# Pairs of steps share their VectorE instructions, the parts of a transform alternate, and a row is written later

## The chip, the cores and the metric

The kernel runs on one core of a Trainium2 chip. The metric is the device time of the execution in microseconds, lower is better. PE is TensorE (the matrix engine), DVE is VectorE, ACT is ScalarE, POOL is GpSimd, SP is SyncE, which here only issues DMAs. L480 is line 480 of the kernel before.

## The reference

A two-dimensional Fourier transform of x (batch 8, sequence 3008, width 256), of which the real part is kept, and a feed-forward layer with a squared relu on all 8 x 3008 = 24064 tokens:

```python
X = np.fft.fft(x, axis=1)
X = np.fft.fft(X, axis=2)
x = X.real.astype(np.float32).reshape(B * S, D)     # 24064 x 256
h = np.maximum(x @ w_in, 0.0)                       # 24064 x 2048
return (h * h @ w_out).astype(np.float32)           # 24064 x 256
```

## The kernel before

The transform along the width is folded into w_in ahead of the main work: gh[:, 0] and gh[:, 1] are the cosine and sine transforms of w_in (2048 columns in 16 chunks of 128), gh[:, 2] is what turns one into the other sign. So the first product takes two inputs of the sequence transform, zc (cosine, part 0) and zs (sine, part 1), with 128 rows (half of the width) on the partitions and tokens as columns. One column stands for two tokens, the token and its mirror: for one the cosine and sine products are added, for the other they are subtracted. Of width index 128 only a row is left over; it stands in row 0 of zs.

**Windows and steps.** The columns are cut into 25 windows (240, 512, 376, 376, 512, 448, then 512 each, the last 360). The loop over windows `for w` (L679) runs eight steps a window, of two chunks of w_in (256 columns) each. Two forms of a step exist:
- A whole step: `pq` (L725, four matmuls of lines L729 and L730) fills a PSUM tile ph; ACT writes its relu to h1 (L739; there are three h1 buffers) and DVE squares it into h2 (L744), or ACT does (L742). Then `turn` (L732, matmuls L735) changes ph to the mirrored tokens, and relu and square follow again.
- A halved step: `half_q` (L750, matmuls L754) makes the sine product alone, which ACT copies, scaled by -2, to sn (L757). `row_sum` (L769) multiplies the spread row eb by two weights (L774, twice) and adds them to sn (L779). `half_p` (L759, matmuls L763) adds the cosine product, and ACT copies the sum to hd (L766). In the next step `halves` (L782) makes the other sign by hd + sn (L787, mirrored), the maximum with 0 of both (L788), and the square of both into h2 (L789).

A plan (L60, read by `halved` and `plan`) names which steps of a window are halved: 1 to 5, 1 to 4 or 1 to 3, by what else the window has to do; windows 0, 1, 2 and 4 have none. In all, 82 steps are halved. sn uses two buffers in turn, hd the tags tt and tm in turn with two buffers each.

**What runs beside the steps.** `others(s)` (L792) is called in the middle of each step, between its first and its second product on PE. It issues three things: jobs that fold the input of a later batch (mostly DVE), a share of the second product of the window before (`ffn2_steps`, 16 matmuls L618 a step, h2 by w_out; every second step ACT evicts a tile to osb, L633, and SP stores it, L598), and a share of the sequence transform of the next window's columns.

That transform comes in units (batch, e), e = 0 or 1. `z_steps` (L460) gives the jobs of a unit by part (0 for zc, 1 for zs) and half (0 or 1). Each job is one matmul (L480). Both halves of a part go to the same PSUM tile pz: half 0 ends with an ACT copy of pz to es (L485); half 1 begins by overwriting pz and ends with an ACT copy of the plus columns to zc or zs (L489), after which DVE makes the mirrored columns, 2 es - pz (L496, `minus`). A half has 3 jobs where e = 0; where e = 1 it has 4 in part 0 and 6 in part 1. The jobs are listed at L721 in the order (part, half) = (0,0), (1,0), (1,1), (0,1), and spread evenly over the steps lo to hi - 1, usually 0 to 6.

**The row.** `row_spread` (L574) sends row 0 of zs to a DRAM row zr by a DMA of the ACT queue (L579) and from there, spread over 128 partitions, to eb by a DMA of the SP queue (L581). It is called in the window before the one that uses eb, in step hi - 1 (usually 6), when the next window has halved steps.

The order on every engine is the one in which the code issues the instructions; the two PSUM tags of the steps and of pz have two buffers each.

Of the kernel before, what the change touches and what calls it, by code (L numbers as in the profile page):

```python
# [8 lines left out]
F32 = mybir.dt.float32  # L9
# [10 lines left out]
def rev_dim(ap, i):  # L20

    dims = [list(d) for d in ap.ap]
    step, cnt = dims[i]
    dims[i] = [-step, cnt]
    return bass.AP(tensor=ap.tensor, offset=ap.offset + step * (cnt - 1), ap=dims)
# [3 lines left out]
def kernel(  # L29
# [27 lines left out]
    FIRST = [240, 512, 376, 376, 512, 448]  # L57
    R23 = float(2.0 ** 23)

    PLAN = {0: ((1, 2, 3, 4, 5), (0, 6, 7)), 1: ((1, 2, 3, 4), (0, 5, 6)), 2: ((1, 2, 3), (0, 5, 6))}  # L60

    RQ = (1, 3, 5, 0, 2, 4)

# [143 lines left out]
    def table_steps(e):  # L207

        n = unit_cols[e][0]
        nr = 2 if e else 3  # L210
        cos_t = const.tile([P, 2 if e else R, n], F16, name=f"cos{e}")
        sin_t = const.tile([P, 2 if e else R, n], F16, name=f"sin{e}")
        tabs[e] = (cos_t, sin_t)
        vec, vs = (evec, evs) if e else (nvec, nvs)
        st = {}

        def row(h, j):
            return j if e else RQ[3 * h + j]

        def freq():  # L220
            kf = st["kf"] = tmp.tile([P, NE], F32, name="kf", tag="kf")[:, 0:n]
            i = 0
            for k0, kstep, cnt in unit_runs[e][0]:
                nc.vector.tensor_scalar(out=kf[:, i : i + cnt], in0=irow[:, i : i + cnt], scalar1=float(kstep), scalar2=float(k0 - kstep * i), op0=ALU.mult, op1=ALU.add)
                i += cnt

        def args(h):
            t = st["t", h] = tmp.tile([P, 3, NE], F32, name="t", tag="tt")
            for j in range(nr):
                r = row(h, j)  # L230
                if e == 0:
                    nc.scalar.activation(t[:, j, 0:n], st["kf"], AF.Copy, bias=R23, scale=vs[:, r : r + 1])
                else:
                    nc.vector.tensor_scalar(out=t[:, j, 0:n], in0=st["kf"], scalar1=vs[:, r : r + 1], scalar2=R23, op0=ALU.mult, op1=ALU.add)

        def turns(h):
            t = st["t", h]
            nc.vector.tensor_scalar(out=t[:, 0:nr, 0:n], in0=t[:, 0:nr, 0:n], scalar1=-R23, scalar2=-float(S), op0=ALU.add, op1=ALU.mult)

        def mods(h):  # L240
            m = st["m", h] = tmp.tile([P, 3, NE], F32, name="m", tag="tm")
            for j in range(nr):
                r = row(h, j)
                nc.vector.scalar_tensor_tensor(out=m[:, j, 0:n], in0=st["kf"], scalar=vec[:, r : r + 1], in1=st["t", h][:, j, 0:n], op0=ALU.mult, op1=ALU.add)

        def absm(h):
            nc.vector.tensor_scalar(out=st["t", h][:, 0:nr, 0:n].bitcast(I32), in0=st["m", h][:, 0:nr, 0:n].bitcast(I32), scalar1=0x7FFFFFFF, scalar2=None, op0=ALU.bitwise_and)

        def sins(h):
            nc.scalar.activation(sin_t[:, 3 * h : 3 * h + nr, :], st["m", h][:, 0:nr, 0:n], AF.Sin, bias=0.0, scale=wk)  # L250

        def coss(h):
            if e:
# [272 lines left out]
    def run(*jobs):  # L526
        for j in jobs:
            j()
# [45 lines left out]
    def row_spread(w):  # L574

        wn = wins[w][1]
        t = eb[w] = tmp.tile([P, WN], F16, name="eb", tag="kf")
        zr = drp.tile([1, WN], F16, name="zr", tag="zr")
        nc.scalar.dma_start(out=zr[0:1, 0:wn], in_=zwin(w)[1][0:1, 0:wn])  # L579
        src = zr[0:1, 0:wn]  # L580
        nc.sync.dma_start(out=t[:, 0:wn], in_=bass.AP(tensor=src.tensor, offset=src.offset, ap=[[0, P], [1, wn]]))  # L581
# [90 lines left out]
    def halved(w):  # L672

        return plan(w)[0]
# [4 lines left out]
    for w in range(NW):  # L679
# [38 lines left out]
        zj, zl = [], []  # L718
        for u in need[w + 1]:
            zu = z_steps(u)  # L720
            zj += [(zu, 0, 0), (zu, 1, 0), (zu, 1, 1), (zu, 0, 1)]  # L721
        f2 = ffn2_steps(*old) if old else []
        phs = {}

# [18 lines left out]
                return []  # L743
            return [lambda: nc.vector.tensor_tensor(h2[:, 2 * s : 2 * s + 2, sg * wn : (sg + 1) * wn], hv, hv, op=ALU.mult)]  # L744

        two = halved(w)
        by_act = plan(w)[1]
        sns, hds = {}, {}

        def half_q(s):  # L750
            ph = phs[s] = ps_h.tile([P, 2, 512], F32, name="ph", tag="psh")
            for a in range(2):
                f0 = (2 * s + a) * P
                nc.tensor.matmul(ph[:, a, 0:wn], gh[:, 1, f0 : f0 + P], zsw[:, 0:wn], start=True, stop=True)  # L754
            i = ROT[0] % 2
            sn = sns[s] = const.tile([P, 2, 2, WN], F16, name=f"sn{i}", tag=f"w16_{i}")
            nc.scalar.activation(sn[:, 0, :, 0:wn], ph[:, :, 0:wn], AF.Copy, bias=0.0, scale=-2.0)  # L757

        def half_p(s):  # L759
            ph, sn = phs[s], sns[s]  # L760
            for a in range(2):
                f0 = (2 * s + a) * P
                nc.tensor.matmul(ph[:, a, 0:wn], gh[:, 0, f0 : f0 + P], zcw[:, 0:wn], start=False, stop=True, skip_group_check=True)  # L763
            hd = tmp.tile([P, 2, 2 * WN], F16, name="hd", tag=("tt", "tm")[ROT[0] % 2])
            ROT[0] += 1
            nc.scalar.activation(hd[:, :, 0:wn], ph[:, :, 0:wn], AF.Copy, bias=0.0, scale=1.0)  # L766
            hds[s] = hd

        def row_sum(s):  # L769

            sn = sns[s]

            def row(a):
                nc.vector.tensor_scalar(out=sn[:, 1, a, 0:wn], in0=eb[w][:, 0:wn], scalar1=wv[:, 2 * s + a : 2 * s + a + 1], scalar2=None, op0=ALU.mult)  # L774

            return [
                lambda: row(0),
                lambda: row(1),
                lambda: nc.vector.tensor_tensor(sn[:, 0, :, 0:wn], sn[:, 0, :, 0:wn], sn[:, 1, :, 0:wn], op=ALU.add),  # L779
            ]  # L780

        def halves(s):  # L782

            sn, hd = sns[s], hds[s]
            hv = hd[:, :, 0 : 2 * wn]
            return [
                lambda: nc.vector.tensor_tensor(rev_dim(hd[:, :, wn : 2 * wn], 2), hd[:, :, 0:wn], sn[:, 0, :, 0:wn], op=ALU.add),  # L787
                lambda: nc.vector.tensor_scalar(out=hv, in0=hv, scalar1=0.0, scalar2=None, op0=ALU.max),  # L788
                lambda: nc.vector.tensor_tensor(h2[:, 2 * s : 2 * s + 2, 0 : 2 * wn], hv, hv, op=ALU.mult),  # L789
            ]  # L790

        def others(s):  # L792
# [13 lines left out]
        ng = 2 if w == 0 or wins[w - 1][1] < 384 < wn else 1  # L806
        for s0 in range(0, NST, ng):
            ss = range(s0, s0 + ng)
            left = halves(s0 - 1) if s0 - 1 in two else []
            if s0 in two:  # L810
                half_q(s0)
                for j in [j for p in zip(left or [run] * 3, row_sum(s0)) for j in p]:
                    j()
                others(s0)
                half_p(s0)
                continue
            for s in ss:
                pq(s)
            for s in ss:
                run(*(left[0:2] + square(s, 0) + left[2:3]))  # L820
            if s0 == hi - 1 and ng == 1 and w + 1 < NW and halved(w + 1):
                row_spread(w + 1)
            others(s0)
            for s in ss:
                turn(s)
            for s in ss:
                run(*square(s, 1))
            for s in ss[1:]:
                others(s)
            if s0 < hi <= s0 + ng - 1 and w + 1 < NW and halved(w + 1):  # L830
                row_spread(w + 1)
# [33 lines left out]
```

## Time and profile before

| | |
|---|---|
| median of 3 runs | 620.66 us (619.44 to 620.81) |
| the profiled execution | 619.07 us |
| its span in the profile | 617.1 us |
| granted TensorE clock | 0.998 |
| window 13 (313.07 to 338.93): length, busy PE / DVE / ACT | 25.86, 24.77 / 20.72 / 22.39 us |
| window 14 (338.93 to 363.01) | 24.08, 24.08 / 19.14 / 21.37 us |
| window 22 (532.91 to 558.19) | 25.28, 23.85 / 21.20 / 21.49 us |

A window begins with its first product's first matmul and ends with the next window's. Window 13 transforms a unit with e = 1 for a later window and has halved steps 1 to 3; window 14 transforms one with e = 0 and has halved steps 1 to 5; window 22 transforms the last unit, e = 1, which window 23 needs at once, and has steps 1 to 5 halved too. Busy times are sums of durations and can overlap at their ends. In lines of the timeline, the first number is the start in microseconds from the span's start, the second the time that the instruction took (for several, from the first to the last), and the bracket at the end is the idle time of the engine before it and what ended it.

### The profile page before, as it was taken

How to read it: one execution, taken by the hardware profiler on the slowest of the kernel's cores; microseconds unless marked ns; L12 is line 12 of the kernel's file. 1: busy time of each engine (PE TensorE's matmuls, PEld its weight loads, DVE VectorE, ACT ScalarE, POOL GpSimd, SP SyncE). 2: the span in 40 equal slices, each digit the busy share in tenths (PEclk: the TensorE clock that was granted, in tenths of full speed). 3: DMA queues.
4: the chain of work that ended last, by engine and by line, in shares of the span. 5: the costliest groups of instructions: out<-in, count | busy, mean ns of one | idle time of the engine just before them, and what ended most of it. 6: DMA issues, size and time to landing. Idle time of an engine off the chain costs nothing.

```text
span 617.1 us, 11655 instructions
## 1 busy us (share of the span) xinstructions
PE 587.7 (95%) x4400; PEld 424.0 (69%) x4400; DVE 498.6 (81%) x870; ACT 517.6 (84%) x673; POOL 77.3 (13%) x125
## 2 busy tenths in 40 slices
PE   5899999999899999999999999999999999999996
PEld 2456776776677777677776767677776776766785
DVE  7886688696888887969978799768987698797980
ACT  7786788888889889889898898888987988979871
POOL 5352200002001022020011100211000200100000
PEclk9999999999999999999999999999999999999999
DMA  8937121164214522631145311552212411111122
GB/s 145 219 71 144 61 68 35 43 150 104 52 38 83 151 85 57 134 112 59 37 106 121 91 49 46 98 131 81 52 31 66 111 52 44 55 47 42 58 58 65
DMA packets 39593, 50.22 MB, mean 81 GB/s; under 512 B 4572, under 2 KB 33393, under 8 KB 39537
## 3 DMA queue, kind: packets, MB, share of 16 engines
q0 software_dynamic: 9344, 22.14, 17.9%
q1 hardware_dynamic: 29923, 27.11, 15.3%
q8 instruction: 34, 0.56, 0.4%
q10 hardware_dynamic: 270, 0.23, 0.1%
q14 instruction: 22, 0.18, 0.1%
HBM read 36.29 MB, written 27.86 MB: 104 GB/s over the span
## 4 chain that ended last, share of the span: by engine, by line
PE 57%; ACT 15%; DVE 13%; issue 8%; DMA 5%; POOL 1%; SPq 0%; ACTq 0%; DVEq 0%; POOLq 0%
PE po L618 33%; ACT h L739 7%; PE ph L735 4%; PE ph L763 4%; PE ph L729 4%; PE ph L730 4%; PE ph L754 4%; PE pz L480 2%; DVE hd L787 2%; DMA out_dram<-osb 2%; DVE h L744 2%; ACT osb L633 2%; ACT hd L766 2%; DVE hd L788 2%; DVE sn L779 2%
## 5 line engine op out<-in xcount | busy, mean ns | idle before, releaser
L618 PE MATMUL po<-wout,h 128*128 128x256 f16 (+1 forms) x3024 | 361.7, 273 | 0.0
L618 PEld LDWEIGHTS <-h 128*128 128x128 f16 (+1 forms) x3024 | 296.5, 98 | 71.3
L739 ACT ACTIVATE h<-ph 128x1024 f16<-128x1024 f32 (+4 forms) x236 | 217.0, 961 | 27.4 <-PE ph L735 18.3
L744 DVE TENSOR_TENSOR h<-h 128x1024 f16<-128x1024 f16 (+4 forms) x173 | 109.5, 641 | 67.4 <-ACT h L739 65.3
L766 ACT ACTIVATE hd<-ph 128x1024 f16<-128x1024 f32 (+3 forms) x82 | 81.4, 992 | 28.1 <-PE ph L763 27.3
L789 DVE TENSOR_TENSOR h<-hd 128x2048 f16<-128x2048 f16 (+3 forms) x82 | 96.5, 1177 | 0.4
L729 PE MATMUL ph<-zc,gh 128*128 128x512 f16 (+4 forms) x236 | 85.2, 363 | 1.3 <-ACT h L739 0.5
L730 PE MATMUL ph<-zs,gh 128*128 128x512 f16 (+4 forms) x236 | 85.1, 363 | 0.4 <-ACT zs L489 0.4
L757 ACT ACTIVATE sn<-ph 128x1024 f16<-128x1024 f32 (+3 forms) x82 | 81.2, 991 | 0.4 <-DVE hd L787 0.2
L787 DVE TENSOR_TENSOR hd<-hd,sn 128x1024 f16<-128x1024 f16 (+3 forms) x82 | 54.9, 670 | 20.0 <-ACT hd L766 14.3
L735 PE MATMUL ph<-zs,gh 128*128 128x512 f16 (+4 forms) x236 | 65.4, 363 | 4.8 <-ACT h L739 3.2
L633 ACT ACTIVATE osb<-po 128x512 f32<-128x512 f32 (+3 forms) x95 | 54.6, 579 | 18.2 <-PE po L618 13.2
L742 ACT ACTIVATE h<-h 128x1024 f16<-128x1024 f16 (+3 forms) x63 | 64.8, 1029 | 2.0
L774 DVE TENSOR_SCALAR sn<-eb,wv 128x512 f16<-128x512 f16 (+3 forms) x164 | 54.3, 342 | 4.2 <-DMA eb<-zr 2.8
L779 DVE TENSOR_TENSOR sn<-sn 128x1024 f16<-128x1024 f16 (+3 forms) x82 | 54.5, 664 | 2.2
L788 DVE TENSOR_SCALAR hd<-hd 128x2048 f16<-128x2048 f16 (+3 forms) x82 | 54.7, 667 | 0.7
L763 PE MATMUL ph<-zc,gh 128*128 128x512 f16 (+3 forms) x164 | 47.3, 370 | 1.7 <-ACT sn L757 1.0
L754 PE MATMUL ph<-zs,gh 128*128 128x512 f16 (+3 forms) x164 | 47.4, 370 | 0.0
L730 PEld LDWEIGHTS <-gh 128*128 128x128 f16 x236 | 23.0, 97 | 25.5 <-issue 2.4
L729 PEld LDWEIGHTS <-gh 128*128 128x128 f16 x236 | 23.0, 97 | 24.8 <-DVE zc L496 1.1
L423 POOL COPY xt<-xt 128x2 f16<-128x2 f16 x16 | 6.0, 402 | 212.2 <-DVE xt L406 212.2
L735 PEld LDWEIGHTS <-gh 128*128 128x128 f16 x236 | 22.3, 97 | 13.2 <-issue 7.9
(121 smaller groups left out, 374.2 us busy)
## 6 DMA issues: line engine op xcount, KB each, us to landing
out_dram<-osb SPq DMA_DIRECT2D x77, 128.0 KB
xo<-in_x_dram POOLq DMA_DIRECT2D x7, 768.0 KB
scr<-ev POOLq DMA_DIRECT2D x8, 390.0 KB, 3.3
eb<-zr SPq DMA_DIRECT2D x18, 128.0 KB
rb<-scr POOLq DMA_DIRECT2D x16, 130.0 KB
out_dram<-osb SPq DMA_DIRECT2D x12, 94.0 KB
w<-in_moe_w_in_dram POOLq DMA_DIRECT2D x2, 512.0 KB
wout<-in_moe_w_out_dram POOLq DMA_DIRECT2D x1, 1024.0 KB
```

The costliest lines, as they stand in the source:

```text
L618: nc.tensor.matmul(po[0:m, j * D : (j + 1) * D], h2[:, fc, q : q + m], wout16[:, fc, :], start=(fc == 0), stop=(fc == NFC - 1))
L729: nc.tensor.matmul(ph[:, a, 0:wn], gh[:, 0, f0 : f0 + P], zcw[:, 0:wn], start=True, stop=False)
L730: nc.tensor.matmul(ph[:, a, 0:wn], gh[:, 1, f0 : f0 + P], zsw[:, 0:wn], start=False, stop=True)
L735: nc.tensor.matmul(phs[s][:, a, 0:wn], gh[:, 2, f0 : f0 + P], zsw[:, 0:wn], start=False, stop=True, skip_group_check=True)
L739: nc.scalar.activation(h1[:, :, 0:wn], phs[s][:, :, 0:wn], AF.Relu)
L744: return [lambda: nc.vector.tensor_tensor(h2[:, 2 * s : 2 * s + 2, sg * wn : (sg + 1) * wn], hv, hv, op=ALU.mult)]
L754: nc.tensor.matmul(ph[:, a, 0:wn], gh[:, 1, f0 : f0 + P], zsw[:, 0:wn], start=True, stop=True)
L757: nc.scalar.activation(sn[:, 0, :, 0:wn], ph[:, :, 0:wn], AF.Copy, bias=0.0, scale=-2.0)
L763: nc.tensor.matmul(ph[:, a, 0:wn], gh[:, 0, f0 : f0 + P], zcw[:, 0:wn], start=False, stop=True, skip_group_check=True)
L766: nc.scalar.activation(hd[:, :, 0:wn], ph[:, :, 0:wn], AF.Copy, bias=0.0, scale=1.0)
L787: lambda: nc.vector.tensor_tensor(rev_dim(hd[:, :, wn : 2 * wn], 2), hd[:, :, 0:wn], sn[:, 0, :, 0:wn], op=ALU.add),
L789: lambda: nc.vector.tensor_tensor(h2[:, 2 * s : 2 * s + 2, 0 : 2 * wn], hv, hv, op=ALU.mult),
```

## The change

- The halved steps come in groups of two neighbouring steps, or one at the end. Plan 1 to 5 becomes (1, 2), (3, 4), (5); 1 to 4 becomes (1, 2), (3, 4); 1 to 3 becomes (1, 2), (3). A group has one sn tile and one hd tile of twice the size; ACT still copies step by step. The sum L779 is made once for a group, in its last step, and so are L787 to L789, in the step after its last. The 82 halved steps make 32 pairs and 18 single ones.
- The row products (L774) are written to the upper half of the hd tile, which the mirrored difference overwrites later, instead of sn.
- hd uses the tag tt alone; of the tables made at the start, t and m share one tile.
- The jobs of a unit are listed as (1,0), (0,0), (1,1), (0,1).
- In a window's step hi - 1, `row_spread` is called behind the second relu and square, and no longer ahead of `others`.

```diff
-    PLAN = {0: ((1, 2, 3, 4, 5), (0, 6, 7)), 1: ((1, 2, 3, 4), (0, 5, 6)), 2: ((1, 2, 3), (0, 5, 6))}
+    PLAN = {0: (((1, 2), (3, 4), (5,)), (0, 6, 7)), 1: (((1, 2), (3, 4)), (0, 5, 6)), 2: (((1, 2), (3,)), (0, 5, 6))}
...
-            t = st["t", h] = tmp.tile([P, 3, NE], F32, name="t", tag="tt")
+            tm = tmp.tile([P, 2, 3, NE], F32, name="tm", tag="tt")
+            t, st["m", h] = tm[:, 0], tm[:, 1]
+            st["t", h] = t
...
-            zj += [(zu, 0, 0), (zu, 1, 0), (zu, 1, 1), (zu, 0, 1)]
+            zj += [(zu, 1, 0), (zu, 0, 0), (zu, 1, 1), (zu, 0, 1)]
...
-        two = halved(w)
+        two = {s: g for g in halved(w) for s in g}
...
-            i = ROT[0] % 2
-            sn = sns[s] = const.tile([P, 2, 2, WN], F16, name=f"sn{i}", tag=f"w16_{i}")
-            nc.scalar.activation(sn[:, 0, :, 0:wn], ph[:, :, 0:wn], AF.Copy, bias=0.0, scale=-2.0)
+            g = two[s]
+            if s == g[0]:
+                i = ROT[0] % 2
+                ROT[0] += 1
+                sns[g] = const.tile([P, 2 * len(g), WN], F16, name=f"sn{i}", tag=f"w16_{i}")
+                hds[g] = tmp.tile([P, 2 * len(g), 2 * WN], F16, name="hd", tag="tt")
+            i = 2 * g.index(s)
+            nc.scalar.activation(sns[g][:, i : i + 2, 0:wn], ph[:, :, 0:wn], AF.Copy, bias=0.0, scale=-2.0)
...
-            hd = tmp.tile([P, 2, 2 * WN], F16, name="hd", tag=("tt", "tm")[ROT[0] % 2])
-            ROT[0] += 1
-            nc.scalar.activation(hd[:, :, 0:wn], ph[:, :, 0:wn], AF.Copy, bias=0.0, scale=1.0)
-            hds[s] = hd
+            i = 2 * g.index(s)
+            nc.scalar.activation(hds[g][:, i : i + 2, 0:wn], ph[:, :, 0:wn], AF.Copy, bias=0.0, scale=1.0)
...
-                nc.vector.tensor_scalar(out=sn[:, 1, a, 0:wn], in0=eb[w][:, 0:wn], scalar1=wv[:, 2 * s + a : 2 * s + a + 1], scalar2=None, op0=ALU.mult)
+                nc.vector.tensor_scalar(out=hd[:, 2 * g.index(s) + a, :], in0=eb[w][:, 0:wn], scalar1=wv[:, 2 * s + a : 2 * s + a + 1], scalar2=None, op0=ALU.mult)
...
-                lambda: nc.vector.tensor_tensor(sn[:, 0, :, 0:wn], sn[:, 0, :, 0:wn], sn[:, 1, :, 0:wn], op=ALU.add),
...
+            jobs = [lambda: row(0), lambda: row(1)]
+            if s == g[-1]:
+                jobs.append(lambda: nc.vector.tensor_tensor(sn, sn, hd, op=ALU.add))
+            return jobs
...
-                lambda: nc.vector.tensor_tensor(rev_dim(hd[:, :, wn : 2 * wn], 2), hd[:, :, 0:wn], sn[:, 0, :, 0:wn], op=ALU.add),
+                lambda: nc.vector.tensor_tensor(rev_dim(hd[:, :, wn : 2 * wn], 2), hd[:, :, 0:wn], sn[:, :, 0:wn], op=ALU.add),
                 lambda: nc.vector.tensor_scalar(out=hv, in0=hv, scalar1=0.0, scalar2=None, op0=ALU.max),
-                lambda: nc.vector.tensor_tensor(h2[:, 2 * s : 2 * s + 2, 0 : 2 * wn], hv, hv, op=ALU.mult),
+                lambda: nc.vector.tensor_tensor(h2[:, 2 * g[0] : 2 * g[-1] + 2, 0 : 2 * wn], hv, hv, op=ALU.mult),
...
-            if s0 == hi - 1 and ng == 1 and w + 1 < NW and halved(w + 1):
-                row_spread(w + 1)
             others(s0)
             for s in ss:
                 turn(s)
             for s in ss:
                 run(*square(s, 1))
+            if s0 == hi - 1 and ng == 1 and w + 1 < NW and halved(w + 1):
+                row_spread(w + 1)
```

More of the change, by code (lines that the diff above doesn't have):

```diff
@@ L240, in mods @@
         def mods(h):
-            m = st["m", h] = tmp.tile([P, 3, NE], F32, name="m", tag="tm")
+            m = st["m", h]
             for j in range(nr):
@@ L754, in half_q @@
                 nc.tensor.matmul(ph[:, a, 0:wn], gh[:, 1, f0 : f0 + P], zsw[:, 0:wn], start=True, stop=True)
-            i = ROT[0] % 2
-            sn = sns[s] = const.tile([P, 2, 2, WN], F16, name=f"sn{i}", tag=f"w16_{i}")
-            nc.scalar.activation(sn[:, 0, :, 0:wn], ph[:, :, 0:wn], AF.Copy, bias=0.0, scale=-2.0)
+            g = two[s]
[6 more added lines that the diff above has]
+            nc.scalar.activation(sns[g][:, i : i + 2, 0:wn], ph[:, :, 0:wn], AF.Copy, bias=0.0, scale=-2.0)
         def half_p(s):
-            ph, sn = phs[s], sns[s]
+            ph, g = phs[s], two[s]
             for a in range(2):
@@ L763, in half_p @@
                 nc.tensor.matmul(ph[:, a, 0:wn], gh[:, 0, f0 : f0 + P], zcw[:, 0:wn], start=False, stop=True, skip_group_check=True)
-            hd = tmp.tile([P, 2, 2 * WN], F16, name="hd", tag=("tt", "tm")[ROT[0] % 2])
-            ROT[0] += 1
-            nc.scalar.activation(hd[:, :, 0:wn], ph[:, :, 0:wn], AF.Copy, bias=0.0, scale=1.0)
-            hds[s] = hd
+            i = 2 * g.index(s)
+            nc.scalar.activation(hds[g][:, i : i + 2, 0:wn], ph[:, :, 0:wn], AF.Copy, bias=0.0, scale=1.0)
         def row_sum(s):
-            sn = sns[s]
+            g = two[s]
+            sn, hd = sns[g][:, :, 0:wn], hds[g][:, :, wn : 2 * wn]
             def row(a):
-                nc.vector.tensor_scalar(out=sn[:, 1, a, 0:wn], in0=eb[w][:, 0:wn], scalar1=wv[:, 2 * s + a : 2 * s + a + 1], scalar2=None, op0=ALU.mult)
-            return [
-                lambda: row(0),
-                lambda: row(1),
-                lambda: nc.vector.tensor_tensor(sn[:, 0, :, 0:wn], sn[:, 0, :, 0:wn], sn[:, 1, :, 0:wn], op=ALU.add),
-            ]
+                nc.vector.tensor_scalar(out=hd[:, 2 * g.index(s) + a, :], in0=eb[w][:, 0:wn], scalar1=wv[:, 2 * s + a : 2 * s + a + 1], scalar2=None, op0=ALU.mult)
[3 more added lines that the diff above has]
+            return jobs
         def halves(s):
-            sn, hd = sns[s], hds[s]
+            if s not in two or s != two[s][-1]:
+                return []
+            g = two[s]
+            sn, hd = sns[g], hds[g]
             hv = hd[:, :, 0 : 2 * wn]
             return [
-                lambda: nc.vector.tensor_tensor(rev_dim(hd[:, :, wn : 2 * wn], 2), hd[:, :, 0:wn], sn[:, 0, :, 0:wn], op=ALU.add),
+                lambda: nc.vector.tensor_tensor(rev_dim(hd[:, :, wn : 2 * wn], 2), hd[:, :, 0:wn], sn[:, :, 0:wn], op=ALU.add),
                 lambda: nc.vector.tensor_scalar(out=hv, in0=hv, scalar1=0.0, scalar2=None, op0=ALU.max),
-                lambda: nc.vector.tensor_tensor(h2[:, 2 * s : 2 * s + 2, 0 : 2 * wn], hv, hv, op=ALU.mult),
+                lambda: nc.vector.tensor_tensor(h2[:, 2 * g[0] : 2 * g[-1] + 2, 0 : 2 * wn], hv, hv, op=ALU.mult),
             ]
@@ L808 @@
             ss = range(s0, s0 + ng)
-            left = halves(s0 - 1) if s0 - 1 in two else []
+            left = halves(s0 - 1)
             if s0 in two:
                 half_q(s0)
-                for j in [j for p in zip(left or [run] * 3, row_sum(s0)) for j in p]:
-                    j()
+                rows = row_sum(s0)
+                run(*(left[0:1] + rows[0:1] + left[1:2] + rows[1:2] + left[2:3] + rows[2:3]))
                 others(s0)
```

## The prediction

> **What bounds the kernel now.** Read first: the busy shares, then the times of whole windows, then the table of waits, then the timeline around each wait that lasts.
>
> ```profile
> span 617.1 us, 11655 instructions
> PE 587.7 (95%) x4400; PEld 424.0 (69%) x4400; DVE 498.6 (81%) x870; ACT 517.6 (84%) x673; POOL 77.3 (13%) x125
> ```
>
> TensorE is the bound on average, at a granted clock of 0.998, so a faster VectorE alone buys nothing; only a gap on PE, or a new one, moves the time.
>
> ```profile
> PE pz L480 <- ACT es L485: 7.6, 9, 1.0
> DVE hd L787 <- ACT hd L766: 14.3, 17, 1.0
> ACT osb L633 <- DMA zr<-zs: 1.8, 1, 1.8
> ```
>
> The one wait of PE that returns is nine times L480 behind L485; the hd wait below it is VectorE's own idleness. Window 13 shows the place (start, duration, engine and line; the bracket is idle time and releaser):
>
> ```profile
> 324.11 0.25 PE L480 MATMUL pz<-cos,spn 128*128 128x94 f16 x2
> ...
> 324.31 0.60 ACT L633 ACTIVATE osb<-po 128x512 f32<-128x512 f32 x1 [0.24 <-PE po L618]
> 324.81 0.48 ACT L485 ACTIVATE es<-pz 128x377 f32<-128x377 f32 x1
> ...
> 325.34 0.24 PE L480 MATMUL pz<-sin,xt 128*128 128x188 f16 x1 [0.98 <-ACT es L485]
> ```
>
> Both halves of part 1 stand next to each other in step 3. The second writes the tile that es copies, and that copy stands behind the 0.60 us eviction. By the start-to-start time of such a matmul (0.09) PE could have gone on near 324.20: 1.145 lost. The same is found near 177.3, 250.8, 397.6, 471.0 and 544.0 (windows 7, 10, 16, 19, 22), at smaller width (0.74) in windows 3 and 4, and 0.75 near 50.9.
>
> VectorE works through the halved steps and falls behind there. Window 14, five halved steps, at its end:
>
> ```profile
> 361.40 0.68 DVE L787 TENSOR_TENSOR hd<-hd,sn 128x1024 f16<-128x1024 f16 x1
> 362.11 0.69 DVE L788 TENSOR_SCALAR hd<-hd 128x2048 f16<-128x2048 f16 x1
> ...
> 362.84 1.23 DVE L789 TENSOR_TENSOR h<-hd 128x2048 f16<-128x2048 f16 x1
> ...
> 363.87 1.25 PE L618 MATMUL po<-wout,h 128*128 128x256 f16 x10
> ```
>
> The last square of window 14 ends at 364.07. The second product of window 14 begins at 363.87, in window 15, with chunk 0; step 5's first chunk is its eleventh matmul (these start 0.109 apart), at 363.87 + 10 x 0.109 = 364.96. So this chain has 0.89 us in hand, and no more.
>
> **Part 1, parts alternate.** The jobs now run (1,0), (0,0), (1,1), (0,1): at 512 columns 20 jobs over seven steps (2, then 3 each), so half 0 of part 1 ends in step 2 of the seven, half 1 starts in the next, and es has a step's time. Gains: windows 7, 10, 13, 16, 19 at 1.145 = 5.73; window 4 0.74; window 1 about 0.5 of 0.75 (its jobs all stand in one step, so some wait may stay). Windows 3 and 22 are left out here (below). Units with three jobs a half never waited there. What hides the change: no copy is added, ACT has the same ones, earlier by one.
>
> **Part 2, one instruction for two steps.** Sums, differences, maxima and squares of 32 pairs of steps merge (18 steps stay single): 4 x 32 = 128 VectorE instructions fewer, no others changed in number. Rows of the groups kept apart by shape, where the wide instruction already occurs:
>
> ```profile
> L744 DVE TENSOR_TENSOR h<-h 128x1024 f16<-128x1024 f16 x128 | 87.0, 688 | 52.0 <-ACT h L739 51.8
> L789 DVE TENSOR_TENSOR h<-hd 128x2048 f16<-128x2048 f16 x69 | 84.0, 1218 | 0.3
> L788 DVE TENSOR_SCALAR hd<-hd 128x2048 f16<-128x2048 f16 x69 | 47.4, 687 | 0.6
> ```
>
> A pair's sum and difference have the shape of the second row: 1.22. Its maximum (4096 wide) is estimated at 0.687 + 2048 x 0.26 ns (slope between the 1504 row, 546 ns, and this one) = 1.22; its square at 1.218 + 2048 x 0.52 ns (slope of the first two rows) = 2.28. In a busy stretch starts follow 0.08 closer than durations say (L789 to L779 1.13), so 1.14, 1.14, 1.14 and 2.2. Two singles take 2 x 0.61, 2 x 0.61, 2 x 0.61 and 2 x 1.13: 0.08 saved by each merger, about 0.3 us per pair, 10 us of VectorE. Bounds for a pair's difference, maximum and square with the two row products of 0.26 between them: 4.7 (each merger saves the whole 0.15 by which two durations exceed one) to 5.7 (two full durations, nothing saved: 1.38 + 1.38 + 2.44 + 0.52); I take 5.0, nearer the rows of the same shape.
>
> This alone would hand PE nothing. But the pair's difference needs the hd copy of its second step, so VectorE starts later. In window 14 the first difference stood at 346.43; now it waits for
>
> ```profile
> 348.18 1.02 ACT L766 ACTIVATE hd<-ph 128x1024 f16<-128x1024 f32 x1 [0.87 <-PE ph L763]
> ```
>
> and starts at 349.25. From 346.43 to the last square's end VectorE had 17.64 us with no idle time. Of that, the second step's row products (0.52) and its sum (0.79) are now done before 349.25, and seven mergers lie after it (0.56): 349.25 + 17.64 - 0.52 - 0.79 - 0.56 = 365.02, 0.95 later than before and 0.1 beyond 364.96; with the semaphore about 0.2 lost. This is windows 11, 14, 17, 20: 0.8. The same sum elsewhere:
> - Window 23 has no z jobs; its last square ends at 583.0, wanted at 581.99 + 10 x 0.109 = 583.08. It will end near 583.7: 0.65.
> - Window 22 feeds the next window at once, through zc behind the last square:
>
> ```profile
> 557.97 0.60 DVE L496 SCALAR_TENSOR_TENSOR zc<-es,pz 128x16 f16<-128x16 f32 x2
> ...
> 558.19 0.39 PE L729 MATMUL ph<-zc,gh 128*128 128x512 f16 x1
> ```
>
>   First difference 540.41, now 543.05: 543.05 + 17.56 - 1.87 = 558.74, and 0.22 to PE: 558.96 against 558.19. The removed stall gives nothing here, and 0.8 is lost.
> - Window 3 likewise at 376 columns: difference 81.43, now 83.75; 83.75 + 13.88 - 1.66 = 95.97 for zc, 0.35 to PE: 0.65 lost, its 0.74 not gained.
> - Windows with three or four halved steps have a whole step behind the last pair, in which VectorE waits for ACT (L744 idle 51.8): nothing lost.
>
> If that cover fell short, the relus would wait for their h1 buffers (three), and turn and the next first product behind them.
>
> A rule speaks against this part: the Trainium skill, Perfetto Trace Analysis, "Optimizing Scalar/DVE Operations", gives about 60 ns of overhead per VectorE instruction on SBUF, says that grouping helps a saturated engine, and advises breaking instructions up where an unsaturated one makes bubbles elsewhere. An estimate by its figure is 0.06 instead of 0.08 per merger: seven windows would end 7 x 0.02 = 0.14 later each, and the sum would be 3.6 instead of 4.6. VectorE at 81% is the second case of its rule, which is the second rival.
>
> **Part 3, the row's write.** L579 (ACT queue) and L581 (SP) move from ahead of step 6's second product to behind its second square, past the osb eviction, the z copies and the second relu. In window 6 it costs today: L633 stood 1.78 behind it, since zs was not yet there (162.22), and turn began 1.73 late at 165.75. Afterwards the relu waits for none of it, but zs itself comes later with the pair (near 163.8), and VectorE with it: I take +0.5, between 0 and 1.7. Elsewhere the write leaves 1 to 2 us later; the row products that need it are in the next window's step 1, over 2 us behind the landing today, and their sum now stands a step later: 0. SP's stores behind L581 wait for nobody here. Without that cover the first sum would be late by up to 2 us, in 18 windows at worst.
>
> **Sum.** 5.73 + 0.74 + 0.5 + 0.5 = 7.5 gained, 0.8 + 0.65 + 0.8 + 0.65 = 2.9 lost: 4.6 less. Span 617.1 gives 612.5, and with the 1.97 outside it 614.5 against the profiled run's 619.07. The median of the runs is 620.66, 1.6 above that run: 616.0 forecast.
>
> **The rivals.**
> 1. VectorE loses nothing at the window ends, since a merger saves 0.15. For it: duration rows; against it: starts overlap. Then 7.5 + 1.145 + 0.74 = 9.4: 611.3.
> 2. Slower: the late start of the pairs decides. Each 0.1 us by which the windows 3, 11, 14, 17, 20, 22, 23 end VectorE later goes to PE seven times, while the gain is 7.5 once. At 0.66 more per window (a pair at 5.33 instead of 5.0) it turns; at 1.0 more (5.5) losses are 9.9: 623.1. For it: nothing in hand in those seven; against it: the same shape's row. The Trainium skill's rule above is this case.
> 3. ACT takes the stall's place: 22.39 of window 13's 25.86 us busy, so 24.7 us would be 91%, with the hd copy and first relu queued behind es. If half of the z stalls (6.5) returns as waits for ACT, 4.25 - 2.9 = 1.3: 619.3. Against it: es is earlier, not longer.
> 4. It does not do what it says: tiles shared by a pair, or the row's late write, chain its steps, and the gains are eaten: 620.7. Against it: a row product needs only eb, and both buffers of a pair's tiles are free steps before.
>
> **How the numbers follow.** Within 0.2% (1.24 us, what a measurement can tell from no change) is 619.4 to 621.9. Forecast 0.45, rival 1 0.17, rival 2 0.20, rival 3 0.13, rival 4 0.05. Faster: 0.43 of the forecast, 0.17, half of rival 3 = 0.66; same: 0.02 + 0.07 + 0.05 + 0.01 of rival 2 = 0.15; slower 0.19. The range 611.0 to 621.5 reaches into rivals 1 and 2 and leaves out about half of the one and most of the other; the forecast's own is 613.5 to 618.5.
>
> **What would show it.** Right: L480 waits for L485 no more (7.6 to below 1.5); VectorE busy about 20 us less by durations (128 x 0.15), 10 us by starts; L789 at 128x4096 near 2.28; first difference of window 14's place about 2.8 us later in its window and the last square about 1 us later; windows 13 and 16 near 24.7 long; L633 without the wait for zr. Wrong: new waits of L618 for L789 above 0.5 each (rival 2), L739 or L763 waiting for ACT (rival 3), L774 or the sum waiting for eb in every window.

## The result and the profile after

| | before | after |
|---|---|---|
| median of the runs, us | 620.05 (619.21 to 620.81, 4 runs) | 613.67 (613.02 to 614.95, 4 runs) |
| profiled execution: time / span | 619.07 / 617.1 | 614.29 / 612.4 |
| first product of window 0 begins at | 21.69 | 23.41 |
| from there to the last matmul's start | 589.82 | 583.87 |

The ratio is 0.990, with a 95% interval of 0.9875 to 0.9925: 6.4 us less by the medians, where 4.6 were forecast (616.0; the range was 611.0 to 621.5). The start of the first product lies between 21.65 and 23.41 in all the profiles of this study, whatever the kernel, so the comparisons below go from the first product to the last matmul: 5.95 us less.

The page of the changed kernel, busy shares (its line numbers are higher: L480 is now L482, L485 is L487, L618 is L620, L774 is L780, L787 to L789 are L795 to L797):

```profile
span 612.4 us, 11453 instructions
PE 586.7 (96%) x4400; PEld 423.4 (69%) x4400; DVE 486.7 (79%) x742; ACT 518.0 (85%) x673; POOL 83.3 (14%) x125
```

128 VectorE instructions are gone and 11.9 us of its busy time (17.3 by the sum of all durations); PE and ACT have what they had within 1 us. The table of waits (waiting line, what it waits for: us in all, times, longest), first two lines from before, then those of the changed kernel:

```profile
DVE sn L774 <- DMA eb<-zr: 2.8, 2, 2.2
...
PEld L729 <- DVE zc L496: 1.1, 2, 0.7
```

```profile
DVE hd L795 <- ACT hd L772: 12.1, 20, 0.8
...
DVE hd L780 <- DMA eb<-zr: 5.8, 3, 2.6
...
PEld L731 <- DVE zc L498: 3.8, 2, 2.1
...
PEld L620 <- DVE h L797: 2.5, 5, 1.3
```

The 7.6 us of L480 behind L485 have no line any more. Three waits have grown: VectorE's for eb from 2.8 to 5.8, the first product's for zc from 1.1 to 3.8, and the second product's for the square (2.5), which did not exist. The stall's place in window 13, on PE:

```profile
319.15 0.21 PE L482 MATMUL pz<-cos,spn 128*128 128x95 f16 x1
319.19 0.24 PE L482 MATMUL pz<-cos,xt 128*128 128x188 f16 x1
319.27 0.24 PE L482 MATMUL pz<-sin,xt 128*128 128x188 f16 x1
319.36 0.59 PE L770 MATMUL ph<-zc,gh 128*128 128x512 f16 x2
```

Half 0 of part 1 ends with the first line (its last matmul, on spn), and half 0 of part 0 begins with the second, 0.04 behind, in another tile. Half 1 of part 1 comes a step later. (Half 1 adds to what half 0 left in pz and does not overwrite it: in the kernel only the first matmul of half 0 has `start`. Either way it must not write before es is copied, so the wait is the same.)

The end of window 14 has moved as the prediction reckoned under part 2. The last square ends 26.17 behind the window's start, where it was 25.14, and the second product (16 matmuls, from 360.59) now takes 2.10 instead of 1.91, since it waits 0.18 for that square:

```profile
360.58 1.23 DVE L797 TENSOR_TENSOR h<-hd 128x2048 f16<-128x2048 f16 x1
...
360.59 2.10 PE L620 MATMUL po<-wout,h 128*128 128x256 f16 x16
```

At the end of window 22 the next window's first product stands behind zc, as forecast:

```profile
553.43 0.60 DVE L498 SCALAR_TENSOR_TENSOR zc<-es,pz 128x16 f16<-128x16 f32 x2
...
553.65 0.39 PE L731 MATMUL ph<-zc,gh 128*128 128x512 f16 x1 [1.21 <-DVE zc L498]
```

### The profile page after: what moved, and what is told of

Its sections match the earlier page's. It is cut to its first block, busy times and chain, and to the rows that moved or that the text cites. A ratio compares the mean times of both kernels' runs of the same rounds, so it can differ in the third digit from the quotient of the medians.

```text
span 612.4 us, 11453 instructions
## 1 busy us (share of the span) xinstructions
PE 586.7 (96%) x4400; PEld 423.4 (69%) x4400; DVE 486.7 (79%) x742; ACT 518.0 (85%) x673; POOL 83.3 (14%) x125
## 4 chain that ended last, share of the span: by engine, by line
PE 63%; DVE 16%; ACT 8%; issue 6%; DMA 5%; POOL 1%; SPq 0%; ACTq 0%; DVEq 0%; POOLq 0%
PE po L620 37%; PE ph L737 5%; PE ph L770 5%; PE ph L731 4%; PE ph L732 4%; PE ph L756 4%; ACT h L741 4%; DVE h L797 3%; DVE hd L795 3%; DVE hd L796 3%; DMA out_dram<-osb 3%; PE pz L482 3%; ACT hd L772 2%; DMA w<-in_moe_w_in_dram 1%; DVE sn L784 1%
## 5 line engine op out<-in xcount | busy, mean ns | idle before, releaser
L620 PE MATMUL po<-wout,h 128*128 128x256 f16 (+1 forms) x3024 | 362.5, 273 | 1.1 <-DVE h L797 1.0
L620 PEld LDWEIGHTS <-h 128*128 128x128 f16 (+1 forms) x3024 | 296.3, 98 | 73.5 <-DVE h L797 2.5
L746 DVE TENSOR_TENSOR h<-h 128x1024 f16<-128x1024 f16 (+4 forms) x173 | 108.0, 641 | 52.0 <-ACT h L741 49.8
L797 DVE TENSOR_TENSOR h<-hd 128x4096 f16<-128x4096 f16 (+7 forms) x50 | 91.7, 1835 | 0.4
L784 DVE TENSOR_TENSOR sn<-sn,hd 128x2048 f16<-128x2048 f16 (+7 forms) x50 | 49.9, 997 | 31.3 <-ACT sn L764 30.0
L635 ACT ACTIVATE osb<-po 128x512 f32<-128x512 f32 (+3 forms) x95 | 54.6, 578 | 17.1 <-PE po L620 15.1
L795 DVE TENSOR_TENSOR hd<-hd,sn 128x2048 f16<-128x2048 f16 (+7 forms) x50 | 49.9, 998 | 14.3 <-ACT hd L772 12.1
L780 DVE TENSOR_SCALAR hd<-eb,wv 128x512 f16<-128x512 f16 (+3 forms) x164 | 51.5, 352 | 5.8 <-DMA eb<-zr 5.8
L796 DVE TENSOR_SCALAR hd<-hd 128x4096 f16<-128x4096 f16 (+7 forms) x50 | 49.9, 997 | 0.7
```

The costliest lines, as they stand in the source:

```text
L620: nc.tensor.matmul(po[0:m, j * D : (j + 1) * D], h2[:, fc, q : q + m], wout16[:, fc, :], start=(fc == 0), stop=(fc == NFC - 1))
L797: lambda: nc.vector.tensor_tensor(h2[:, 2 * g[0] : 2 * g[-1] + 2, 0 : 2 * wn], hv, hv, op=ALU.mult),
```

## The experiments

All runs in one table: length of a window from its first product to the next window's (24: to the last matmul's start), in us, from each run's profile. Windows not shown differ by at most 0.1 from before in runs 1 to 7 and 10, but for window 9 of run 2 (25.40).

| window | before | after | 1 order | 2 pairs | 3 row | 4 order, row | 5 mixed | 6 late singles | 7 zc first | 10 best |
|---|---|---|---|---|---|---|---|---|---|---|
| 1 | 22.00 | 21.52 | 21.53 | 22.00 | 22.00 | 21.52 | 21.52 | 21.52 | 21.52 | 21.60 |
| 3 | 20.03 | 20.65 | 19.98 | 20.49 | 20.03 | 19.99 | 19.99 | 20.28 | 19.00 | 19.02 |
| 4 | 23.08 | 22.12 | 22.12 | 22.85 | 23.08 | 22.12 | 22.12 | 22.12 | 22.59 | 22.57 |
| 6 | 25.47 | 24.94 | 25.47 | 27.03 | 23.60 | 23.61 | 23.61 | 24.36 | 23.61 | 23.61 |
| 7 | 25.37 | 24.22 | 24.22 | 26.80 | 25.36 | 24.22 | 24.22 | 24.22 | 24.22 | 24.22 |
| 10, 13, 19 | 25.86 | 24.61 | 24.61 | 25.86 | 25.86 | 24.61 | 24.61 | 24.61 | 24.61 | 24.61 |
| 16 | 25.86 | 24.61 | 24.74 | 25.86 | 25.86 | 24.61 | 24.61 | 24.61 | 24.61 | 24.61 |
| 17 | 24.08 | 24.08 | 24.85 | 24.08 | 24.14 | 25.64 | 24.08 | 24.08 | 24.08 | 24.08 |
| 22 | 25.28 | 26.53 | 24.98 | 26.49 | 25.28 | 24.98 | 25.15 | 25.48 | 23.90 | 23.91 |
| 23 | 23.18 | 22.33 | 23.18 | 22.85 | 22.66 | 22.67 | 22.33 | 22.33 | 22.81 | 22.81 |
| 24 | 30.14 | 31.30 | 30.14 | 31.29 | 30.14 | 30.14 | 30.47 | 30.78 | 30.47 | 30.48 |
| all, first to last | 589.8 | 583.9 | 582.8 | 595.5 | 587.5 | 581.0 | 579.7 | 581.4 | 578.4 | 578.5 |

| run | median, us | before beside it | ratio, 95% interval |
|---|---|---|---|
| 1 order | 611.88 | 619.93 | 0.9867 (0.9847 to 0.9887) |
| 2 pairs | 624.25 | 619.93 | 1.0073 (1.0054 to 1.0092) |
| 3 row | 616.12 | 619.93 | 0.9940 (0.9926 to 0.9955) |
| 4 order, row | 609.21 | 619.93 | 0.9828 (0.9811 to 0.9845) |
| 5 mixed | 609.32 | 619.35 | 0.9839 (0.9825 to 0.9853) |
| 6 late singles | 610.52 | 619.35 | 0.9864 (0.9846 to 0.9882) |
| 7 zc first | 607.55 | 619.35 | 0.9815 (0.9800 to 0.9830) |
| 8 more halved, mixed | 614.48 | 619.35 | 0.9918 (0.9904 to 0.9931) |
| 9 more halved, singles | 610.03 | 619.27 | 0.9842 (0.9821 to 0.9864) |
| 10 best | 607.68 | 619.27 | 0.9807 (0.9789 to 0.9825) |
| 11 pairs, slow row | 626.02 | 619.27 | 1.0096 (1.0069 to 1.0123) |
| 12 singles, slow row | 624.78 | 619.27 | 1.0074 (1.0049 to 1.0099) |

**1. The order alone**, in the kernel before:

```diff
-            zj += [(zu, 0, 0), (zu, 1, 0), (zu, 1, 1), (zu, 0, 1)]
+            zj += [(zu, 1, 0), (zu, 0, 0), (zu, 1, 1), (zu, 0, 1)]
```

> The kernel before with the new order of the transform's jobs alone. Theory (the order makes the whole gain, the pairs only cost): windows 7, 10, 13, 16, 19 are 1.25 us shorter each (25.86 to 24.61 in window 13), window 4 by 0.85, window 1 by 0.5; windows 3 and 22 stay as they are (20.0 and 25.3), because there zc behind VectorE's last square sets the next window's first product, with or without the stall. In all 7.6 us less, ratio 0.988, more than the whole change gave without the start. Rival (the pairs' relief of VectorE is what lets the order pay): less than 4 us less, with new waits for VectorE in windows 7 to 19.

As expected: five windows 1.12 to 1.25 shorter, window 4 0.96, window 1 0.47, window 3 unchanged. Two windows were not foreseen: 22 is 0.30 shorter, and 17 is 0.77 longer, since VectorE waits 2.2 for a late eb there. From first to last the order alone gives 7.1 us, more than the whole change (5.95).

**2. The pairs alone**: the changed kernel with that line and the place of `row_spread` as they were before.

> The changed kernel with the old order of jobs and the old place of the row's write: the pairs alone. Theory: slower by 2.5 to 4.5 us, ratio 1.004 to 1.007: the nine waits of L482 for the copy L487 stay (7.6 us); window 3 0.6 longer, window 22 1.2 to 2.4 longer (both through zc), window 6 0.5 to 1.5 longer (the row's write waits for a zs that comes later, ahead of eviction and relu), windows 11, 14, 17, 20 as before. Rival (10 us less of VectorE pays by itself): 1 to 3 us faster, spread over the windows with halved steps.

Slower, as expected, by 0.73%; from first to last it is 5.7 us, more than the 2.5 to 4.5 named. Two windows were missed: window 7 is 1.4 longer and window 9 0.45. What the pairs save on VectorE did not pay. In window 6 the eviction L635 stands 3.1 us behind the row's write, which waits for the late zs, and PE then stands still for 3.2 us. Right behind that, from 168.38 to 172.00, the granted TensorE clock is 0.53, and matmuls of 512 columns start 0.427 apart instead of 0.217. By these distances the slow stretch cost some 1.6 us (an estimate), which accounts for the 1.4 of window 7. So about 4 of the 5.7 us are waits of the pairs, and the rest is the slow clock behind the longest of them.

**3. The row's write alone**, in the kernel before:

```diff
-            if s0 == hi - 1 and ng == 1 and w + 1 < NW and halved(w + 1):
-                row_spread(w + 1)
             others(s0)
...
                 run(*square(s, 1))
+            if s0 == hi - 1 and ng == 1 and w + 1 < NW and halved(w + 1):
+                row_spread(w + 1)
```

> The kernel before with the row's write moved alone. Theory: window 6 1.6 us shorter (25.47 to about 23.9; the relu no longer stands behind the row's DMA and turn of step 7 begins about 1.7 earlier), all other windows within 0.1: 1.6 less, ratio 0.9974. Rival (the place matters to the rows of the next windows too): windows 7 to 23 change, and waits of L774 for eb appear.

Window 6 gains 1.87, where 1.6 was expected. ACT there, in this run's timeline (lines numbered as before):

```profile
161.54 0.48 ACT L489 ACTIVATE zc<-pz 128x376 f16<-128x376 f32 x1
161.90 1.03 ACT L739 ACTIVATE h<-ph 128x1024 f16<-128x1024 f32 x1
162.53 0.22 ACTq L579 DMA_DIRECT2D zr<-zs  x1
162.85 1.02 ACT L739 ACTIVATE h<-ph 128x1024 f16<-128x1024 f32 x1
```

The write meets a zs that is ready and no longer holds eviction, zc copy and relu. Window 23 gains 0.52, which was not expected: before, PE waits 0.27 and 0.31 for ScalarE in it, and in this run a wait of 0.69 for zc at its start, where it was 0.07, covers both. In the changed kernel the write still meets a zs that isn't ready, because the pairs bring it late, and it holds a relu for 1.26 (its timeline of ACT):

```profile
162.76 1.02 ACT L741 ACTIVATE h<-ph 128x1024 f16<-128x1024 f32 x1
164.72 0.22 ACTq L581 DMA_DIRECT2D zr<-zs  x1
165.04 1.02 ACT L741 ACTIVATE h<-ph 128x1024 f16<-128x1024 f32 x1 [1.26 <-DVE zs L498]
```

The move is not worth less there: with the pairs window 6 is 27.03 without it (run 2) and 24.94 with it. It is the pairs that cost 1.3 in this window even so.

**4. Order and row without the pairs**: both diffs above.

> The whole change without its pairs: order and row's write. Theory: the sum of the two, 9.0 us less than before (span near 608 if it starts as early as before), 2 to 3 us faster than the whole change, ratio 0.985. Rival (pairs needed): between the order alone and the whole change, slower than 0.990.

8.8 us less from first to last, by the medians 10.7, and faster than the whole change. Only window 17 is worse, by 1.56: there eb lands late (line 774, VectorE), and ACT's sn copy, which has two tiles, waits for VectorE two steps on:

```profile
412.16 0.62 DVE L774 TENSOR_SCALAR sn<-eb,wv 128x512 f16<-128x512 f16 x2 [2.97 <-DMA eb<-zr]
```

**5. Mixed.** In the changed kernel, windows 3, 6, 22 and 23 make sum, difference, maximum and square step by step again, on the halves of the pair's tiles:

```diff
-            if s == g[-1]:
+            i = 2 * g.index(s)
+            if w in (3, 6, 22, 23):
+                jobs.append(lambda: nc.vector.tensor_tensor(sn[:, i : i + 2], sn[:, i : i + 2], hd[:, i : i + 2], op=ALU.add))
+            elif s == g[-1]:
...
-            if s not in two or s != two[s][-1]:
+            if s not in two or (s != two[s][-1] and not (w in (3, 6, 22, 23))):
                 return []
...
-            sn, hd = sns[g], hds[g]
+            sn, hd, f0, f1 = sns[g], hds[g], 2 * g[0], 2 * g[-1] + 2
+            if w in (3, 6, 22, 23):
+                i = 2 * g.index(s)
+                sn, hd, f0, f1 = sn[:, i : i + 2], hd[:, i : i + 2], 2 * s, 2 * s + 2
...
-                lambda: nc.vector.tensor_tensor(h2[:, 2 * g[0] : 2 * g[-1] + 2, 0 : 2 * wn], hv, hv, op=ALU.mult),
+                lambda: nc.vector.tensor_tensor(h2[:, f0:f1, 0 : 2 * wn], hv, hv, op=ALU.mult),
```

> The whole change, but with single instructions per step in windows 3, 6, 22 and 23 (tiles still shared by two steps). Theory (pairs cost only where the next window waits for VectorE's last work, and where the row's write waits for a late zs): window 3 20.65 to 20.0, window 6 24.94 to 23.6, window 22 26.53 to 25.0, window 23 22.33 to 22.7, and the wait of 1.15 in window 24 for the last square goes; all others as in the whole change, window 17 at 24.1: from the first product to the last matmul 579.5 (whole change 583.9), ratio to before 0.981. Rival (pairs cost everywhere): no better than the change without pairs (581.0 in its profile, of which 1.5 in window 17).

579.66 against 579.5 expected. Beside run 4, which has no pairs, only windows 17, 22, 23 and 24 differ by more than 0.03: -1.56, +0.17, -0.34 and +0.33. So outside the four windows and the tail the pairs cost nothing here. The last two are one loss in two places: PE's wait of 0.35 for ACT's sn copy in window 23 is gone, and 0.32 stands at the square in window 24 instead; the two windows together are 52.81 and 52.80.

**6. Late singles.** The changed kernel, where each pair instruction is two of one step, in the same place of the queue (sum, maximum and square are changed in the same way as the difference, which is shown):

```diff
...
-                lambda: nc.vector.tensor_tensor(rev_dim(hd[:, :, wn : 2 * wn], 2), hd[:, :, 0:wn], sn[:, :, 0:wn], op=ALU.add),
+                lambda: [nc.vector.tensor_tensor(rev_dim(hd[:, k : k + 2, wn : 2 * wn], 2), hd[:, k : k + 2, 0:wn], sn[:, k : k + 2, 0:wn], op=ALU.add) for k in ks],
...
```

> The whole change, with the pairs' sums, differences, maxima and squares at the same late places, but each as two instructions of one step. Theory (the late start is the cost, and a merger gives 0.08 back): last squares of the windows with five halved steps end 0.5 later than with pairs; window 22 0.3 to 0.6 longer (26.9), window 3 0.4 longer (21.0), the wait at the start of windows 12, 15, 18, 21 grows from 0.18 to 0.7 and their length by 0.2 to 0.5; 2 to 3.5 us slower than the whole change, ratio to before 0.994. Rival (a wide instruction costs as much as two): the same as the whole change within 0.5.

Both theories failed: it is faster than the whole change, 581.4 against 583.9 from first to last. VectorE in window 22 of this run, in the timeline:

```profile
533.24 0.68 DVE L796 TENSOR_TENSOR hd<-hd,sn 128x1024 f16<-128x1024 f16 x1
534.53 0.69 DVE L796 TENSOR_TENSOR hd<-hd,sn 128x1024 f16<-128x1024 f16 x1 [0.61 <-ACT hd L772]
...
536.88 2.35 DVE L798 TENSOR_TENSOR h<-hd 128x2048 f16<-128x2048 f16 x2
```

The same window of the changed kernel:

```profile
537.32 1.22 DVE L795 TENSOR_TENSOR hd<-hd,sn 128x2048 f16<-128x2048 f16 x1 [0.68 <-ACT hd L772]
...
540.12 2.28 DVE L797 TENSOR_TENSOR h<-hd 128x4096 f16<-128x4096 f16 x1
```

Reckoned from the window's start (524.52 and 527.12), two narrow differences end at 10.70, one wide one at 11.42: the first narrow one runs while the second step's copy is still under way. The squares show what a merger saves: two take 2.35 from end to end, one takes 2.28. So the merged difference waits for the last of its inputs and gives up about 0.7, and a merger gets back 0.07. A whole pair gets back no more than that: in window 14 the second pair, from the start of its sum to the end of its square, takes 6.42 merged and 6.49 in this run. A wide difference begins 1.33 behind the start of the wide sum that it needs, and two narrow ones begin 1.20 behind the start of two narrow sums.

**7. zc first.** Run 5, and in windows 3 and 22 the square of step 5 goes behind step 6's transform jobs:

```diff
-                run(*(left[0:2] + square(s, 0) + left[2:3]))
+                run(*(left[0:2] + square(s, 0) + ([] if w in (3, 22) and s == 6 else left[2:3])))
             others(s0)
+            if w in (3, 22) and s0 == 6:
+                run(*left[2:3])
```

> As the run with single instructions in windows 3, 6, 22, 23, and in windows 3 and 22 the square of step 5 goes behind step 6's transform jobs, so that zc's minus does not stand behind it. Theory (zc sets the next window's first product there): window 3 0.9 shorter (19.1), window 22 1.15 shorter (23.8), nothing given back in windows 4 and 23, since the square ends before its chunk is wanted: 2.0 us less than that run. Rival (another wait is right behind): under 0.7 less.

Windows 3 and 22 give 0.99 and 1.25, as expected. That nothing would be given back was wrong: windows 4 and 23 take 0.47 and 0.48, so 1.28 is left where 2.0 was expected.

**8. More halved steps.** Run 5 with a fourth halved step where the plan has three:

```diff
-2: (((1, 2), (3,)), (0, 5, 6))}
+2: (((1, 2), (3, 4)), (0, 5, 6))}
```

> As the run with single instructions in windows 3, 6, 22, 23, and the ten windows with three halved steps get a fourth, as pairs (1, 2), (3, 4): two matmuls less each, 0.43 us of PE. If the 10 us that pairs save on VectorE can be spent: 4.3 us less than that run. If VectorE or ACT is the bound in those windows after all: less than 1 us less, or slower, with waits of PE for L741 or L797 in windows 10, 13, 16, 19.

Slower than run 5 by 5.3 (584.93): windows 12, 15 and 18 are 0.37 shorter, but window 9 is 1.52 longer, 13, 16 and 19 are 0.9 to 1.3 longer, and 6, 8, 11, 14 and 20 0.4 to 0.5. In window 9 zs again holds the row's write, as in window 6.

**9. The same with single instructions everywhere.**

> The run with a fourth halved step in ten windows, but with single instructions in all windows. Theory (VectorE is the bound there, by length and by late starts): where VectorE is busy almost without a break, the mergers' 0.08 is worth something and the pairs' wait for the second copy costs less than elsewhere, so the two are close: first product to last matmul 583 to 587, against 584.9 with pairs. Rival (a pair costs its wait everywhere): 581 or less. Other rival (the 10 us that pairs save is what carries such a plan): 588 or more.

580.29, 4.6 less than with pairs, and under 581 as the first rival had it. Windows 8, 10, 12, 13 and 15 are 0.33 to 0.39 shorter than in run 5; window 18, where a late row's wait arrives, and window 19 are 0.8 and 1.2 longer. VectorE is busier here (518.5 us) than in run 8 (508.0).

**10. Run 7 with single instructions in window 24 too.**

> The run with single instructions in windows 3, 6, 22, 23 and zc ahead of the square in 3 and 22, with single instructions in window 24 too. Theory: the wait of 0.32 in window 24 goes; first product to last matmul 578.05 instead of 578.4, ratio to before about 0.981, the fastest of all so far.

No gain over run 7 (578.48 against 578.38): the wait of 0.32 in window 24 stays. It is a wait for the last square of window 23, which has single instructions in run 7 already; single ones in window 24 can't bring it earlier. The two are the fastest, 5.4 to 5.5 less than the changed kernel from first to last.

**11 and 12. A slow row**, with pairs (the whole change) and without (run 4):

```diff
+        zr2 = drp.tile([1, WN], F16, name="zr2", tag="zr2")
+        nc.sync.dma_start(out=zr2[0:1, 0:wn], in_=zr[0:1, 0:wn])
-        src = zr[0:1, 0:wn]
+        src = zr2[0:1, 0:wn]
```

> The whole change with one more DMA in the row's way (zr to a second DRAM row, and from there to eb, both on SP's queue), so that eb lands some 2 us later. Theory (with pairs the row is wanted only by the sum in the pair's second step): 0 to 1.5 us slower than the whole change (583.9). Rival (no more slack than with single steps): as much slower as the kernel without pairs.

> Order and row's write without the pairs, with the same DMA more in the row's way. Theory: the first step's sum waits for eb in several windows and the 0.7 to 1.6 of window 17 is found again: 2 to 6 us slower than the same kernel without that DMA (581.0, with 1.56 in window 17). Rival: under 1 us slower, then window 17 was something else.

Both lose 15 us (598.6 against 583.9, 596.0 against 581.0 from first to last), so neither expected size came, and the delay was larger than meant. In windows 17 and 19 eb was issued 5.4 to 6.3 later than without it. SP issued nothing in between: it waited 4.5 to 5.5 for the added transfer of one row. Why that took so long there is not shown; for window 10 of run 11 eb was issued 1.8 behind the added transfer's own issue (242.46 and 244.29).

The lengths hold more than these waits. Behind waits of PE of 3.8 and 4.5 us in window 5, and in windows 18 and 23 (run 11) and 19 (run 12), the granted clock is 0.50 to 0.51 for 3 to 5 us. By the matmuls' distances that is some 5.7 us in run 11 and 3.9 in run 12 (estimates). So the two sums can't be compared as costs of the row alone.

In window 17 VectorE waits 5.3 and 5.4 for the row. With single tiles that window is 28.07 instead of the 24.08 of before; with pairs it keeps its 24.08, and the next one is 4.2 longer, of which about 1.5 is the slow clock. Two-step tiles move the cost of a late row and may lessen it; they don't remove it.

## Why the prediction was right

The direction and the mechanism of the gain held, and so did most terms. One mechanism failed (the loss in the four windows), and the sum came as close as it did because misses offset each other. Term by term, windows of the changed kernel against before:

| term | forecast | measured |
|---|---|---|
| windows 7, 10, 13, 16, 19, stall | -5.73 | -6.15 |
| window 4 | -0.74 | -0.96 |
| window 1 | -0.5 | -0.48 |
| window 6, row | -0.5 | -0.53 |
| windows 11, 14, 17, 20, last square | +0.8 | 0.0 |
| window 3, zc | +0.65 | +0.62 |
| window 22, zc | +0.8 | +1.25 |
| windows 23 and 24, last square | +0.65 | +0.31 (-0.85 and +1.16) |
| sum | -4.6 | -5.9 |

- **The order** was right, and run 1 shows it alone. It was mis-sized by a tenth of a microsecond in four windows: with the 1.145 a gap of 0.11 before L763, a wait for ACT, went too. The stall was not "the one wait of PE that returns": the same table has L735 behind ACT's L739, 3.2 us in six waits. Such waits for ACT are what the next points turn on.
- **The four windows 11, 14, 17 and 20** are the term that failed. The square did come late (1.03, forecast 0.95) and PE did wait 0.18 (forecast 0.2), but a wait is not yet a loss: PE waits for ACT in the first two steps behind it anyway. Before, these waits were 0.11 and 0.31; after, PE waits 0.18 for the square and 0.22 for ACT; window 15 is 23.46 long either way. Run 7 shows the same from the other side: what zc first gained came back as 0.24 and 0.31 of such waits in window 23, which a stall ahead of them had covered.
- **Window 22** was mis-sized: VectorE's first difference came 10.20 behind the window's start (forecast 10.14), but zc's last columns began 26.31 behind it instead of 25.83. The second pair's difference started only 1.69 behind its sum, where window 14 has 1.33. The durations of a pair's difference, maximum and square were right (1.23, 1.22, 2.29 measured; 1.22, 1.22, 2.28 estimated). That each merger gives 0.08 back was not: between a sum and the difference that needs it the starts are 1.33 apart, and not 1.14.
- **Windows 23 and 24**: the last square made PE wait 1.15, forecast 0.65. The 0.85 that window 23 gave was not forecast: three waits of PE for ACT in it (0.27, 0.31, 0.35) went, two of them behind a longer wait for zc (1.37 instead of 0.07) that is counted in window 22. Not foreseen were thus 0.8 less in the four windows and 0.85 less here, against 0.45 more in window 22 and 0.5 more in window 24. That the sum still came near is luck.
- **What the pairs cost** was put down to the late start, and run 6 narrows that: the place in the queue costs less than the merger, which makes one instruction wait for both steps. Run 6 is 2.5 faster than the whole change; beside run 4 it is 0.3 slower, and 1.9 slower if window 17 is left out. The Trainium skill (Perfetto Trace Analysis, "Optimizing Scalar/DVE Operations") says that where such an engine isn't saturated but makes bubbles on others, breaking up instructions may let work complete sooner. Runs 6 and 9 agree, by 2.5 and 4.6 us. Its figure of about 60 ns an instruction agrees with the 0.07 between two squares and one; 0.08 was taken.
- **The row** came out as taken in window 6 (0.53, taken 0.5 out of a range of 0 to 1.7, so the size is partly luck) and was wrong in its cover: "over 2 us behind the landing" did not hold before the change either. VectorE stood before the row products in windows 5, 17 and 19 (0.6, 1.3 and 2.2; the profile puts the 1.3 down to nothing, so that it was eb is likely and not shown). In window 19 the transfer is issued as late as 1.9 into the window that uses it, right behind stores. The changed kernel waits 1.4, 1.8 and 2.6 there, and none of the three windows is longer than before: the pair's sum stands later.

The three parts alone sum to -7.1 + 5.7 - 2.4 = -3.8 from first to last, the whole change to -5.9. The difference is mostly 1.4 in window 7, where run 2 has the slow clock, 0.8 of window 17 in run 1 and 0.45 of window 9 in run 2. Without the pairs it is -8.8, with 1.56 of window 17 in it. Rival 2's mechanism, that late pairs are paid by PE at the ends of a few windows, is real and weighs some 4 us (the whole change against run 5); the order's gain is larger. Its sign, a wait of the second product for the square above 0.5, came once, with 1.15 in window 24.

Left open: why the second difference in window 22 begins 0.46 behind the end of the sum it needs, where window 14 has 0.10 (0.45 in run 2); and window 17 in runs 1 and 4, where the time at which eb was there (6.6 and 7.2 after its issue, 5.9 in the changed kernel) was not controlled.

## What to carry to other kernels

Merge instructions on an engine only if their inputs come at the same time, or if that engine is the bound: here a merged square saved 0.07 us and a merged difference waited 0.7. Price the parts of a change apart, and test them apart: one edited line brought more than the whole gain, and the pairs took 3 to 4 us back (the whole change against runs 4 and 5). Before a new wait is counted as a loss, look at which engine paces the next steps, since a wait there already may absorb it.

## What the hardware showed that was not expected

A transfer of one row to 128 partitions, issued on a queue that also carries stores, took 4.1 to 7.2 us from issue to the first instruction that waited for it (windows 5, 17 and 19 of the changed kernel and run 4). Its issue can stand behind stores as well: in window 19 of the changed kernel the issue of one store took 4.70 (from 452.75), and eb went at 457.56, 2.2 into the window. One more transfer of one row ahead of it made eb's issue up to 6.3 us later (run 12, window 17), of which SP waited 4.5 for that transfer.

A long wait of PE can cost more than its length. Behind waits of 3.2 (run 2), 3.8 (run 11) and 4.5 us (run 12) matmuls started twice as far apart for 3 to 5 us, at a granted clock of 0.50 to 0.53. Behind one of 2.5 (run 12, window 17) they did not, and in the kernels before and after, whose longest waits in the windows are 1.9, no such stretch is found.
